# Attention phase of a fused attention + MoE + MoE kernel: PSUM tiles of one bank for the one-bank steps, and a step order written down as a string

## The chip, the cores and the metric

The kernel runs on one core of one Trainium2 chip. The metric is device microseconds of that core for one execution, the median of the runs shown. Engines are named as in the profile: PE (TensorE matmul), PEld (its weight loads), DVE (VectorE), ACT (ScalarE), POOL (GpSimd) and SP (SyncE, which here only issues DMAs).

## What is computed

Three layers follow each other, all in fp32.

```python
s_g  = scale * q_g @ [k_g, k_l].T                      # 32 global queries see all 544 keys
out_g = softmax(s_g) @ [v_g, v_l]
s_ll = where(|i - j| <= 32, scale * q_l @ k_l.T, -1e9) # 512 local queries: a band of keys
s_l  = [scale * q_l @ k_g.T, s_ll]                     # and the 32 global keys
out_l = softmax(s_l) @ [v_g, v_l]
x = heads of [out_g, out_l] side by side               # 2176 tokens x 512
h = (silu(x @ w_gate) * (x @ w_val)) @ w_out           # d_ff 1536
y = h @ w_in2
out = (y * tanh(softplus(y))) @ w_out2                 # d_ff 2048
```

There are 4 batches, 8 heads of 64 columns, 512 local and 32 global tokens per batch.

## The kernel before, in words

The program has two phases. The change touches only the first, the **attention phase**, which takes the first fifth of the time. It works on pairs of heads: n = 0 to 15, four per batch. All its steps are small tasks with a name, an engine, what they need, and, for PE steps that write PSUM, how many banks they take and which later step frees them (`until`). The steps of one pair are:

- on SP, `qk` (six DMAs, lines 166 to 171) and `v` (four DMAs, lines 190 to 192) load the operands; `gk`, `vg` and `vgb` (lines 157, 177, 181) load the global rows of a batch, `w` (lines 581, 584) a piece of the first weights, `Xd` and `GXd` (line 138) store the result to DRAM;
- `A` (PE, L200, two banks) transposes q and k; `Ak`, `Aq` (L289, L299, L301) and `At`, `Ag` (POOL) copy them out;
- `S`, g = 0 and 1 (PE, L317, two banks) makes the scores of half a pair's queries; four `M` (DVE, L328) add the mask and take the minimum of the negated scores; four `E` (ACT, L335) exponentiate; `R` (DVE, L340 and L341) and `N` (POOL, L346 and L348) normalise;
- `C` (PE, L200 on `sm` and `sng`, two banks) transposes the probabilities, `V` (ACT, L363) copies them out;
- `D` (PE, L381 and L385, one bank) multiplies by the values; `Xc` (ACT, L124), `Xh` (DVE, L134), `Xl` (POOL, L136) and `Xd` split and store the result.

For every second pair the global queries go through the same chain with the names `GA` (PE, L412, one bank), `GM` (DVE, L418 to L420), `GE` (ACT, L425 and L427), `GR`, `GN`, `GT` (PE, two banks), `GV` (ACT, L449), `GO` (PE, L459, one bank), `GXc` (ACT, L128). Per batch `AG` and `GG` (PE, L485 and L501, one bank each) prepare the global keys and queries.

Between these stand six conversions of weight pieces, `Cq`, `Cf` 0 to 3, `Ch`, `Cl` (ACT L588, four DVE steps in `w_step`, ACT, POOL), and work of the second layer that is used as filling for PE: for token tiles 0, 1 and 2 the steps `F` (gate and value products, PE L656, one bank), `Ft`, `Fg`, `Fp`, `Fh`, `Fl`, and then `F2` 0 to 3 (the output product, PE L656, one bank each), whose banks `Fy` (DVE, L709) copies into `y`.

The order of these 872 steps is set by `in_order`, a small list scheduler that runs when the kernel is built: each task has a key (a number from `KEY` plus ten per pair) and an estimated duration (`ROOM`, `LAND`), each engine takes the ready task with the smallest key, and the PSUM is eight banks in four tiles of two. A two-bank step takes a whole tile; a one-bank step takes a free bank, preferring one whose other half is in use:

```python
PAIR = [ps_pair.tile([128, 2, 512], F32, ...) for i in range(4)]
def one(task):
    i = place[task][0]
    return PAIR[i // 2][:, i % 2]
...
got = [min(some, key=lambda i: used[i ^ 1] is None)] if some else None
```

On every engine the instructions then stand in the order in which `in_order` put them, and run in that order. Semaphores between engines are set by the framework from what each instruction reads and writes of each tile. In the built program this is by tile, and not by bank, for waits between PE and its readers: a PE instruction that writes one bank of a `pair` tile waits for the last DVE or ACT read of either bank, and a reader waits for the last PE write to either.

The **second phase** starts with `plain_tile(0, 3)` (PE L1064, first layer of token tile 3) and is laid out by a planner of its own, which the change does not touch. Its DVE, ACT and POOL work begins with the conversion of the next weights (DVE L596 to L602, POOL L894).

Of the kernel before, what the change touches and what calls it, by code (L numbers as in the profile page):

```python
# [1 line left out]

# [18 lines left out]
def tile_attn_moe_moe2(  # L21
# [75 lines left out]
    def setup():  # L97
# [5 lines left out]
        for i in range(7):  # L103
            nc.tensor.matmul(PAIR[3][:, 0, 0:128], lhsT=z, rhs=z, start=True, stop=True)
# [93 lines left out]
    def transpose_half(out, src, j):  # L198
# [6 lines left out]
    LAND = {"Xd": 2.6, "GXd": 2.6, "TD": 2.8, "TO": 3.5, "w": 8.0, "qk": 4.0, "v": 5.0, "gk": 4.5, "vg": 5.0, "vgb": 5.0}  # L205
    QACT = lambda n: n % 2 == 0
    KEY = {'lP': 0.2, 'lO': 0.1, 'qk': -24.4, 'v': -9.4, 'A': -11.6, 'S': 0.5, 'E': 10.4, 'R': 49.5,
           'N': -29.7, 'C': -90.7, 'V': -58.2, 'D': -82.8, 'X': 21.9, 'GA': -4.7, 'GT': 42.8, 'GO': 27.7,
           'gk': -16.2, 'vg': 1.0, 'AG': -11.3, 'w': 24.3, 'dw': 20.7, 'C0': 82.8, 'dC': 3.0, 'F': 80.0,
           'At': -70.0, 'GM': -260.3, 'Ch': -231.6}  # L210
    CT = lambda i: KEY["C0"] + KEY["dC"] * i

    ROOM = {"A": 0.6, "S": 0.85, "M": 0.41, "E": 0.51, "R": 0.55, "N": 1.98, "V": 0.73, "D": 1.95, "Xh": 0.6, "Xl": 1.35,
            "GM": 1.2, "GE": 1.02, "GR": 0.55, "GN": 1.7, "Aq": 0.66, "Ak": 0.72, "Xc": 0.62, "GXc": 0.25, "qk": 3.4, "v": 2.4}
    STEPS = (1.1, 0.6, 0.9, 0.95)

    def task(name, key, engine, room, needs, work, banks=0, until=None):
        room = STEPS[name[2]] if name[0] == "Cf" else ROOM.get(name[0], room)
        tasks[name] = (key, engine, room, [x for x in needs if x is not None], work, banks, until)

    def in_order():

        done, start, order = {}, {}, []
        used = [None] * 8
        free = {"PE": 0.0, "DVE": 2.5, "ACT": 3.9, "POOL": 3.0, "SP": 0.0}
        wait = {e: sorted((n for n in tasks if tasks[n][1] == e), key=lambda n: tasks[n][0]) for e in free}
        now = 0.0
        while any(wait.values()):
            for i in range(8):
                if used[i] is not None and done.get(used[i], 1e9) <= now:  # L230
                    used[i] = None
            for e, queue in wait.items():
                if free[e] > now:
                    continue
                for n in queue:
                    key, _, room, needs, work, banks, until = tasks[n]
                    if any(done.get(x, 1e9) > now for x in needs):
                        continue
                    if banks == 2:
                        got = next(([2 * i, 2 * i + 1] for i in range(4) if used[2 * i] is used[2 * i + 1] is None), None)  # L240
                    elif banks == 1:
                        some = [i for i in range(8) if used[i] is None]
                        got = [min(some, key=lambda i: used[i ^ 1] is None)] if some else None
                    else:
                        got = []
                    if got is None:
                        continue
                    for i in got:
                        used[i] = until
# [295 lines left out]
    def attention():  # L545
# [12 lines left out]
        for name in in_order():  # L558
            tasks[name][4]()
# [886 lines left out]
```

## Time and profile before

| what | us |
|---|---|
| median of 3 runs (lowest, highest) | 951.75 (950.51, 951.76) |
| the profiled execution's own time | 947.95 |
| span of that execution in the profile | 945.9 |
| PE busy | 908.0 (96%) |
| DVE, ACT, POOL busy | 620.7, 582.5, 528.4 (66%, 62%, 56%) |

The profile is of one execution. Its times in the rows are microseconds from the start of the span, unless marked ns. In a timeline row the columns are start, duration, engine, line, operation, output and inputs, shapes and count; in brackets stand the idle time of that engine just before it and the instruction that ended the wait. A "pair" in the rows is any of the four PSUM tiles, since buffer numbers are left out. The first `L1064` at 199.28 marks the end of the attention phase.

### The profile page before, as it was taken

To read this page: it belongs to the slowest core of one execution; us is meant where nothing else is said; L and a number is where in the kernel's file an instruction comes from. 1 tells how busy PE (TensorE), PEld (TensorE's weight loads), DVE (VectorE), ACT (ScalarE), POOL (GpSimd) and SP (SyncE) were. 2 spreads that over 40 slices of the span, in tenths; PEclk is the share of its full clock that TensorE was granted. 3 is DMA by queue.
4 is the path that set the end of the run, shared out by engine and by line. 5 is a ranking of instruction groups with operands and counts; after the bars stand their busy time and mean duration, and the time that the engine had idled before them with its cause. 6 is when DMAs were issued, how large, how long until landed. Compare 5 with 4: busy or idle time off the path is not lost.

```text
span 945.9 us, 16820 instructions
## 1 busy us (share of the span) xinstructions
PE 908.0 (96%) x6166; PEld 814.7 (86%) x6166; DVE 620.7 (66%) x1174; ACT 582.5 (62%) x1218; POOL 528.4 (56%) x512
## 2 busy tenths in 40 slices
PE   8878989989899999999999999999999999999998
PEld 6666767878798999999999998888888889888986
DVE  6676866559978878878788895555755575212323
ACT  6775656733334555454455668878767877776763
POOL 5776766648999568575383697434423352233211
PEclk9989999999999999999999999999999999999999
DMA  6768634346766555666655321112211210000112
GB/s 149 176 161 202 164 101 101 83 139 202 232 231 225 179 184 175 193 196 202 192 192 204 130 66 47 45 49 63 68 45 45 68 54 14 0 1 1 69 43 78
DMA packets 134609, 112.76 MB, mean 119 GB/s; under 512 B 79616, under 2 KB 119552, under 8 KB 134528
## 3 DMA queue, kind: packets, MB, share of 16 engines
q1 hardware_dynamic: 133088, 110.85, 38.6%
q8 instruction: 48, 0.79, 0.3%
q10 hardware_dynamic: 1440, 0.85, 0.3%
q14 instruction: 33, 0.27, 0.1%
HBM read 93.85 MB, written 17.83 MB: 118 GB/s over the span
## 4 chain that ended last, share of the span: by engine, by line
PE 80%; POOL 7%; ACT 4%; DVE 4%; issue 3%; DMA 1%; SPq 1%; POOLq 0%; DVEq 0%; ACTq 0%
PE p L1230 19%; PE p L1185 19%; PE p L1104 17%; PE p L1007 11%; PE pair L656 4%; PE p L1064 2%; POOL b L964 2%; PE pair L381 2%; PE pair L317 1%; PE pair L385 1%; POOL w L894 1%; PE pair L200 1%; POOL a L894 1%; POOL e L846 1%; PE pair L459 1%
## 5 line engine op out<-in xcount | busy, mean ns | idle before, releaser
L894 POOL TENSOR_TENSOR a<-s,a 128x384 fp32r<-128x384 f32 (+2 forms) x125 | 146.7, 1183 | 236.6 <-ACT a L893 210.2
L1230 PE MATMUL p<-w,a 128*128 128x512 f32 x816 | 199.0, 391 | 0.0
L1185 PE MATMUL p<-xh,w 128*128 128x384 f32 (+1 forms) x640 | 189.9, 358 | 0.1
L1230 PEld LDWEIGHTS p<-w,a 128*128 128x128 f32 x816 | 152.5, 188 | 29.8
L1007 PE MATMUL p<-a,w 128*128 128x384 f32 (+2 forms) x744 | 139.3, 335 | 3.0 <-POOL w L894 3.0
L1007 PEld LDWEIGHTS p<-a,w 128*128 128x128 f32 x744 | 126.4, 188 | 6.8 <-POOL w L894 3.3
L1104 PE MATMUL p<-xh,w 128*128 128x384 f32 (+1 forms) x496 | 128.7, 326 | 0.4 <-ACT b L1116 0.4
L1185 PEld LDWEIGHTS p<-xh,w 128*128 128x128 f32 x640 | 118.2, 188 | 12.4 <-DVE s L1208 0.5
L894 POOL TENSOR_TENSOR w<-cx,w 128x512 fp32r<-128x512 f32 (+1 forms) x78 | 95.5, 1233 | 48.1 <-ACT w L893 32.5
L1185 PE MATMUL p<-xl,w 128*128 128x384 f32 (+1 forms) x320 | 114.3, 357 | 0.0
L1208 DVE TENSOR_TENSOR s<-s,p 128x384 f32<-128x384 f32 (+1 forms) x80 | 45.7, 605 | 95.7 <-ACT s L1206 95.2
L893 ACT ACTIVATE a<-s 128x384 fp32r<-128x384 f32 (+2 forms) x142 | 73.7, 537 | 35.3 <-DVE s L1050 34.0
L596 DVE SCALAR_TENSOR_TENSOR fl<-q,st 128x512 f32<-128x512 f32 x68 | 67.6, 993 | 41.4 <-ACT q L588 41.3
L1196 ACT ACTIVATE s<-p 128x384 f32<-128x384 f32 (+1 forms) x80 | 42.2, 528 | 82.7 <-PE p L1185 81.5
L1104 PEld LDWEIGHTS p<-xh,w 128*128 128x128 f32 x496 | 88.4, 188 | 0.8 <-ACT b L1116 0.7
L1104 PE MATMUL p<-xl,w 128*128 128x384 f32 (+1 forms) x248 | 80.7, 326 | 0.0
L1116 ACT ACTIVATE b<-p 128x384 f32<-128x384 f32 (+1 forms) x72 | 34.0, 473 | 68.1 <-PE p L1104 65.7
L1016 DVE TENSOR_TENSOR y<-p,y 128x384 f32<-128x384 f32 (+2 forms) x116 | 62.1, 541 | 18.0 <-PE p L1007 17.4
L602 DVE SCALAR_TENSOR_TENSOR cx<-st,cx 128x512 uint32<-128x512 uint32 x68 | 71.7, 1054 | 0.8
L600 DVE SCALAR_TENSOR_TENSOR cx<-fl,cx 128x512 uint32<-128x512 uint32 x68 | 70.4, 1035 | 1.1
L1064 PE MATMUL p<-xh,w 128*128 128x384 f32 (+1 forms) x224 | 65.3, 364 | 1.2 <-DVE y L709 1.2
L1246 DVE TENSOR_TENSOR y<-p,y 128x512 f32<-128x512 f32 x51 | 34.8, 690 | 48.3 <-PE p L1230 48.1
(135 smaller groups left out, 1773.8 us busy)
## 6 DMA issues: line engine op xcount, KB each, us to landing
st<-in_moe_w_out SPq DMA_DIRECT2D x28, 512.0 KB, 4.6
e<-td SPq DMA_DIRECT2D x32, 384.0 KB, 4.0
st<-in_moe_w_in SPq DMA_DIRECT2D x16, 512.0 KB, 3.5
vw<-in_v_l SPq DMA_DIRECT2D x32, 224.0 KB, 4.5
st<-in_moe_w_gate SPq DMA_DIRECT2D x12, 512.0 KB
st<-in_moe_w_val SPq DMA_DIRECT2D x12, 512.0 KB, 3.4
td<-b SPq DMA_DIRECT2D x16, 384.0 KB, 3.2
xh<-td SPq DMA_DIRECT2D x16, 384.0 KB, 4.7
```

Source lines behind the costliest of these rows:

```text
L596: nc.vector.scalar_tensor_tensor(fl, q, TINY2, hw, op0=ALU.is_ge, op1=ALU.mult)
L600: nc.vector.scalar_tensor_tensor(x, fu, 0xC0000000, x, op0=ALU.bitwise_and, op1=ALU.bitwise_or)
L602: nc.vector.scalar_tensor_tensor(x, STG.pop(p)[:, :, 0], 29, x, op0=ALU.logical_shift_right, op1=ALU.bitwise_or)
L893: add("ACT", AC(n), lambda e: nc.scalar.activation(out=dst(0), in_=src(), func=AF.Copy), r=[rd], w=list(dict.fromkeys(wr)), margin=m)
L894: add(lo or [("POOL", PO(n))], 0, lambda e: vec(e).tensor_tensor(out=dst(1), in0=src(), in1=dst(0).bitcast(F32), op=ALU.subtract), r=[rd, ...
L1007: nc.tensor.matmul(ps.h[:, 0:n], lhsT=a.h[:, d], rhs=b.h[:, 0:n], start=(i == 0 and j == 0), stop=(i == len(ws) - 1 and j == 2))
L1016: add("DVE", DV(n), lambda e: nc.vector.tensor_tensor(out=ya, in0=ps.h[:, 0:n], in1=ya, op=ALU.add), r=[ps], w=yt)
L1064: nc.tensor.matmul(ps.h[:, 0:n], lhsT=a.h[:, d], rhs=b[:, c, c0:c0 + n], start=(c == 0 and j == 0), stop=(c == KD - 1 and j == 2))
L1104: nc.tensor.matmul(ps.h[:, 0:n], lhsT=w.h[:, 256 * a + 128 * c:256 * a + 128 * c + 128], rhs=xs[b][:, c, :], start=(start and c == 0 and j ...
L1185: nc.tensor.matmul(h.h[:, 0:n], lhsT=a.h[:, d], rhs=b[:, c, c0:c0 + n], start=(c == 0 and j == 0), stop=(c == KD - 1 and j == 2))
L1208: add("DVE", DV(n), lambda e, s=s, h=h, n=n: nc.vector.tensor_tensor(out=s.h[:, 0:n], in0=s.h[:, 0:n], in1=h.h[:, 0:n], op=ALU.mult), r=[h ...
L1230: nc.tensor.matmul(ACC_[c].h, lhsT=a.h[:, d], rhs=b.h, start=(first and j == 0), stop=(last and j == 2))
```

## The change

It does four things.

1. PSUM becomes two tiles of two banks (`PAIR`) and four tiles of one bank (`ONE`). Two-bank steps (`A`, `S`, `C`, `GT`: 88 in all) use the first, one-bank steps (`D`, `GA`, `GO`, `AG`, `GG`, `F`, `F2`) the second.
2. `in_order` no longer schedules. It reads a string of 872 letters, each a kind of step, and takes the next step of that kind; the tile of a PE step is the one that has been free longest.
3. Keys, estimated durations and landing times go; the steps themselves, what they need, their engines and their instructions stay the same.
4. The order that the string gives is another one. Conversions of weights and `F` steps stand earlier (the first `F` after the fifth `D`, where before it came after the eighth), the weight loads `w` too, and on SP the `qk` loads of later pairs stand ahead of the `v` loads of earlier ones.

```diff
-            nc.tensor.matmul(PAIR[3][:, 0, 0:128], lhsT=z, rhs=z, start=True, stop=True)
+            nc.tensor.matmul(ONE[0][:, 0:128], lhsT=z, rhs=z, start=True, stop=True)
...
-    PAIR = [ps_pair.tile([128, 2, 512], F32, tag=f"pair{i}", name=f"pair{i}") for i in range(4)]
+    PAIR = [ps_pair.tile([128, 2, 512], F32, tag=f"pair{i}", name=f"pair{i}") for i in range(2)]
+    ONE = [ps_pair.tile([128, 512], F32, tag=f"one{i}", name=f"one{i}") for i in range(8 - 2 * len(PAIR))]
     place = {}
 
     def both(task):
-        return PAIR[place[task][0] // 2]
+        return PAIR[place[task]]
 
     def one(task):
-        i = place[task][0]
-        return PAIR[i // 2][:, i % 2]
+        return ONE[place[task]]
...
-    KEY = {'lP': 0.2, 'lO': 0.1, 'qk': -24.4, 'v': -9.4, 'A': -11.6, 'S': 0.5, 'E': 10.4, 'R': 49.5,
...
+    KINDS = ("qk gk A AG Ak AGk At Aq AGe Ag w S GG M E GA R GGe N C V vg GM v GE GR GN Cq D Cf vgb GT "
+             "Xc GV Xh GO Xl Xd Ch GXc GXh GXd Cl GXl F_g Ft F_v Fg Fp Fh Fl F2 Fy").split()
+    ORDER = "abbcdefghadijkjlamlnnnnnooooocnonoephglqnroacsnonnnooelqjgsohtunnnvbnoqtouwsxkllyaxdonnnnzcoonAeooBnpjCq"
...
-                    if banks == 2:
-                        got = next(([2 * i, 2 * i + 1] for i in range(4) if used[2 * i] is used[2 * i + 1] is None), None)
-                    elif banks == 1:
-                        some = [i for i in range(8) if used[i] is None]
-                        got = [min(some, key=lambda i: used[i ^ 1] is None)] if some else None
...
+        free = {2: list(range(len(PAIR))), 1: list(range(len(ONE)))}
+        until = {}
+        for letter in ORDER:
+            n = left[KINDS[(ascii_letters + digits).index(letter)]].pop(0)
+            _, needs, _, banks, last = tasks[n]
...
+            place[n] = free[banks].pop(0) if banks else None
+            if banks:
+                until[last] = banks, place[n]
+            if n in until:
+                free[until[n][0]].append(until[n][1])
+            done.append(n)
+        return done
...
-        task(("A", n), t + KEY["A"], "PE", 0.65, [("qk", n)], qk, 2, ("Aq", n))
+        task(("A", n), "PE", [("qk", n)], qk, 2, ("Aq", n))
```

Three places show what moves. In the rows below a line number of the changed kernel is 23 to 29 smaller or one larger than that of the same code before (PE L459 is L436 now, L656 is L629, L1064 is L1035, SP L166 is L167).

**PE, around the third global output (`GO`, L459; L436 now).** The `gtl` rows are `GO`, the `pt` rows the end of the fifth `D`, the `kst` rows two `S`. Before:

```order
L385 MATMUL pair1_118<-pt_964,vw_907 64x64 [waits DMAHW3_49]
L385 MATMUL pair1_118<-pt_964,vw_907 64x64 [waits DMAHW4_49]
L385 MATMUL pair1_118<-pt_964,vw_907 64x64 x6
L385 MATMUL pair1_118<-pt_1017,vw_907 64x64 x8
L459 MATMUL pair1_118<-gtl_1082,vw_907 64x32 [waits Activation_49]
L459 MATMUL pair1_118<-gtl_1082,vw_907 64x32 x7
L459 MATMUL pair1_118<-gtl_1082,vgb_116 64x32 [waits DMAHW1_49]
L459 MATMUL pair1_118<-gtl_1082,vgb_116 64x32
```

Now:

```order
L295 MATMUL pair1_118<-kst_1092,qT_1136 128x224 [waits DVE_49,Pool_49]
L295 MATMUL pair1_118<-kst_1092,qT_1136 128x224 x3
L295 MATMUL pair0_117<-kst_1092,qT_1136 128x224 [waits Activation_49]
L295 MATMUL pair0_117<-kst_1092,qT_1136 128x224
L295 MATMUL pair0_117<-kst_1092,qT_1136 128x224 [waits Pool_49]
L295 MATMUL pair0_117<-kst_1092,qT_1136 128x224
L436 MATMUL one2_121<-gtl_1205,vw_927 64x32 x8
L436 MATMUL one2_121<-gtl_1205,vgb_116 64x32 [waits DMAHW5_49]
```

`GO` stood right behind `D` in the other bank of the same tile and waited for ACT, which reads that tile for `D`; now it has a tile of its own, stands behind two `S` steps, and its first rows wait for nothing.

**PE, the end of the attention phase.** These are the last `F2` step (on the `ah` and `al` tiles) and the first matmul of the second phase (on `xh`). Before:

```order
L656 MATMUL pair0_117<-ah_2898,w8_1982 128x384 [waits DVE_49]
L656 MATMUL pair0_117<-al_2899,w8_1982 128x384
L656 MATMUL pair0_117<-ah_2898,w9_1983 128x384
L656 MATMUL pair0_117<-ah_2992,w10_2131 128x384
L656 MATMUL pair0_117<-al_2993,w10_2131 128x384
L656 MATMUL pair0_117<-ah_2992,w11_2132 128x384
L1064 MATMUL p0_3076<-xh_105,w0_1450 128x384 [waits DVE_49,PE_49]
```

Now:

```order
L629 MATMUL one0_119<-ah_2818,w8_2158 128x384 [waits DVE_49]
L629 MATMUL one0_119<-al_2819,w8_2158 128x384
L629 MATMUL one0_119<-ah_2933,w10_2296 128x384
L629 MATMUL one0_119<-al_2934,w10_2296 128x384
L629 MATMUL one0_119<-ah_2933,w11_2297 128x384
L1035 MATMUL p0_3078<-xh_105,w0_756 128x384 [waits PE_49]
```

The four `F2` of token tile 2 used the two banks of `pair0` in turn; now they use `one0`, `one3`, `one1` and `one0` again. The first matmul of the second phase no longer waits for DVE.

**SP, the first loads.** After the loads of pairs 0 and 1. Before:

```order
L190 DMA vw<-in_v_l 128x7x64 x2
L191 DMA vw<-in_v_l 64x2x64
L192 DMA vw<-in_v_l 64x2x64
L166 DMA ks<-in_k_l 128x4x64 x2
L168 DMA qs<-in_q_l 128x3x64 x2
L170 DMA qs<-in_q_l 96x2x64
L171 DMA qs<-in_q_l 32x2x64
L190 DMA vw<-in_v_l 128x7x64 x2
```

Now:

```order
L558 DMA st_197<-in_moe_w_gate 128x4x256
L167 DMA ks<-in_k_l 128x4x64 x2
L169 DMA qs<-in_q_l 128x3x64 x2
L171 DMA qs<-in_q_l 96x2x64
L172 DMA qs<-in_q_l 32x2x64
L167 DMA ks<-in_k_l 128x4x64 x2
L169 DMA qs<-in_q_l 128x3x64 x2
L171 DMA qs<-in_q_l 96x2x64
L172 DMA qs<-in_q_l 32x2x64
L178 DMA vg<-in_v_g 32x4x64 x4
L158 DMA gkq<-in_k_g 128x1x64 x2
L191 DMA vw<-in_v_l 128x7x64 x2
```

The first `v` load stood third and now stands behind a weight load, the `qk` loads of pairs 2 and 3, `vg` and half of a `gk`.

## Rows read from the trace of the kernel before

**Rows 1.** Busy time of PE by stretch: us, PE busy (count), PEclk, DMA share, GB/s

```profile
0.00:48.00 48.00, 40.39 (x624) 1.00 0.69 162
48.00:72.00 24.00, 17.80 (x270) 0.86 0.67 161
72.00:199.20 127.20, 111.09 (x1418) 1.00 0.51 133
```

**Rows 2.** Timeline, one stall of PE and what led to it

```profile
61.25 0.93 PE L381 MATMUL pair<-pt,vg 128*64 128x128 f32 x11 [1.36 <-DMA vg<-in_v_g]
63.26 0.69 DVE L418 TENSOR_REDUCE gmx<-pair 128x1 f32<-128x512 f32 x1 [4.30 <-PE pair L385]
64.36 0.69 ACT L425 ACTIVATE sg<-pair,grc 128x512 f32<-128x512 f32 x1 [3.95 <-DVE rc L340]
65.34 0.58 ACT L124 ACTIVATE xf<-pair 128x512 f32<-128x512 f32 x1
65.98 0.66 PE L459 MATMUL pair<-gtl,vw 128*64 128x32 f32 x16 [2.75 <-ACT xf L124]
```

**Rows 3.** Timeline, other stalls of PE behind readers of the neighbouring bank

```profile
123.22 0.44 PE L656 MATMUL pair<-xh,w 128*128 128x384 f32 x1 [0.32 <-DVE t L674]
152.86 0.44 PE L656 MATMUL pair<-xh,w 128*128 128x384 f32 x1 [0.65 <-ACT gxf L128]
165.57 0.60 ACT L124 ACTIVATE xf<-pair 128x512 f32<-128x512 f32 x1 [1.56 <-PE pair L412]
167.37 0.41 PE L656 MATMUL pair<-xh,w 128*128 128x384 f32 x1 [1.39 <-DVE gmx L419]
191.75 0.44 PE L656 MATMUL pair<-ah,w 128*128 128x384 f32 x1 [0.70 <-ACT xf L124]
```

**Rows 4.** Waits of PE, 72 to 199.2 us: us in total, times, longest

```profile
PE pair L656 <- DVE y L709: 2.9, 4, 0.9
...
PE pair L381 <- DVE y L709: 0.8, 1, 0.8
```

**Rows 5.** A stall of PE on a load, and PE's clock behind two stalls

```profile
51.88 0.46 PE L200 MATMUL pair<-ident,ks 64*128 64x64 f32 x8 [1.71 <-DMA ks<-in_k_l]
52.00:58.00 6.00, 5.84 (x50) 0.72 0.94 225
66.00:72.00 6.00, 6.00 (x122) 0.72 0.56 132
```

**Rows 6.** The first DMA issues, the first D step, and landing times of v loads

```profile
7.92 1.03 SPq L190 DMA_DIRECT2D vw<-in_v_l  x2
10.46 1.06 SPq L166 DMA_DIRECT2D ks<-in_k_l  x2
13.67 1.04 SPq L190 DMA_DIRECT2D vw<-in_v_l  x2
16.10 2.58 SPq L177 DMA_DIRECT2D vg<-in_v_g  x4
28.02 0.43 SPq L584 DMA_DIRECT2D st<-in_moe_w_gate  x1
19.43 1.49 PE L381 MATMUL pair<-pt,vg 128*64 128x128 f32 x15
vw<-in_v_l SPq DMA_DIRECT2D x32, 224.0 KB, 4.5
```

**Rows 7.** Timeline where the second phase begins, and its first stall of PE

```profile
199.28 0.41 PE L1064 MATMUL p<-xh,w 128*128 128x384 f32 x1 [1.21 <-DVE y L709]
199.05 1.89 DVE L596 SCALAR_TENSOR_TENSOR fl<-q,st 128x512 f32<-128x512 f32 x1
250.33 2.08 PE L1007 MATMUL p<-a,w 128*128 128x512 f32 x7 [2.95 <-POOL w L894]
```

**Rows 8.** Costliest groups of the attention phase: readers of the two-bank tiles

```profile
L328 DVE CUSTOM_DVE_ANT_0 sm<-pair,mask 128x224 f32<-128x224 f32 x128 | 42.5, 383 | 3.0 <-PE pair L317 3.0
L363 ACT ACTIVATE pt<-pair 128x640 f32<-128x640 f32 x32 | 21.9, 699 | 3.0 <-PE pair L200 2.9
```

More of the change, by code (lines that the diff above doesn't have):

```diff
@@ L1 @@
 from contextlib import ExitStack
+from string import ascii_letters, digits
 import concourse.bass as bass
@@ L211, in tile_attn_moe_moe2 @@
[L211 to L219, printed above, removed]
@@ L221, in in_order @@
-    def in_order():
[L223 to L238, printed above, removed]
-                    if banks == 2:
-                        got = next(([2 * i, 2 * i + 1] for i in range(4) if used[2 * i] is used[2 * i + 1] is None), None)
-                    elif banks == 1:
-                        some = [i for i in range(8) if used[i] is None]
-                        got = [min(some, key=lambda i: used[i ^ 1] is None)] if some else None
[L244 to L249, printed above, removed]
-                    place[n] = got
-                    late = LAND.get(n[0], KEY["lP"] if e == "PE" else KEY["lO"])
-                    free[e] = now + room
-                    done[n] = now + room + late
-                    order.append(n)
-                    queue.remove(n)
-                    break
-            later = [x for x in list(free.values()) + list(done.values()) if x > now]
-            if not later:
-                raise RuntimeError("no task can start: " + str({e: q[:3] for e, q in wait.items()}))
-            now = min(later)
-        return order
@@ new lines, in tile_attn_moe_moe2, with task @@
+    ORDER += "oqtTFsCHVWtuuXYGxLJCNIZ0O0GIKLZZRK00PLZ0"
+    def task(name, engine, needs, work, banks=0, until=None):
+        tasks[name] = engine, [x for x in needs if x is not None], work, banks, until
+    def in_order():
+        left, done = {}, []
+        for n in tasks:
+            left.setdefault(f"F_{n[3]}" if n[0] == "F" else n[0], []).append(n)
+        free = {2: list(range(len(PAIR))), 1: list(range(len(ONE)))}
[3 more added lines that the diff above has]
+            _, needs, _, banks, last = tasks[n]
+            if not all(x in place for x in needs):
+                raise RuntimeError(f"{n} comes before what it needs")
+            place[n] = free[banks].pop(0) if banks else None
[5 more added lines that the diff above has]
+        return done
@@ L528, in go @@
             next(gen, 0)
-        t = CT(i)
-        task(("Cq", i), t, "ACT", 0.67, [("w", i)] + ([("Cf", i - 1, 0)] if i else []), go)
+        task(("Cq", i), "ACT", [("w", i)] + ([("Cf", i - 1, 0)] if i else []), go)
         for j, room in enumerate((0.70, 1.20, 0.75, 0.80)):
             need = [("Cf", i, j - 1)] if j else [("Cq", i)] + ([("Cf", i - 1, 3), ("Cl", i - 2)][:i] if i else [])
-            task(("Cf", i, j), t + 0.1 * j, "DVE", room, need, go)
-        task(("Ch", i), t + KEY["Ch"], "ACT", 0.63, [("Cf", i, 3)], go)
-        task(("Cl", i), t + KEY["Ch"], "POOL", 1.45, [("Ch", i)], go)
+            task(("Cf", i, j), "DVE", need, go)
+        task(("Ch", i), "ACT", [("Cf", i, 3)], go)
+        task(("Cl", i), "POOL", [("Ch", i)], go)
     TD = {}
@@ L558, in attention @@
         for name in in_order():
-            tasks[name][4]()
+            tasks[name][2]()
     STG, W = {}, {}
@@ L712, in add_fill @@
             before = ("F2", t, c, 0)
-            task(before, key, "PE", 0.15 + n * 0.00272, [("Fl", t, fs[0]), ("Fl", t, fs[1]), ("Cl", 4), ("Cl", 5)],
+            task(before, "PE", [("Fl", t, fs[0]), ("Fl", t, fs[1]), ("Cl", 4), ("Cl", 5)],
                  lambda c=c: [second_part(c, i) for i in range(2)], 1, ("Fy", t, c))
-            key += 1
-            task(("Fy", t, c), key, "DVE", 0.69, [before], lambda c=c: copy(c))
+            task(("Fy", t, c), "DVE", [before], lambda c=c: copy(c))
     def out_rows(c0, n):
```

109 lines of the change are left out of this document (53 added, 56 removed).

## Prediction

> **What bounds the kernel now.** I read the busy times by stretch first, then the waits of PE, then the timeline around the longest of them. PE is not busy for 945.9 - 908.0 = 37.9 us of the span, and most of that lies in the attention phase, as [rows 1] show: in the first 48 us PE is idle for 48.00 - 40.39 = 7.6 us, from 48 to 72 for 6.2 us, from there to the end of the attention phase for 16.1 us, 29.9 us together. PE's work in the phase is the same before and after, so the question is which of these waits the change takes away, and what it puts in their place.
>
> Three kinds of wait matter. The first is of the program's own making. [rows 2] are one chain: a late load of `vg` holds the fifth `D` for 1.36 us; `GM` on DVE, which reads a `GA` result in the *other* bank of D's tile, waits 4.30 us for D's matmuls; `GE` on ACT waits 3.95 us for DVE; behind it on ACT stands `Xc`, D's reader; and PE's next step, `GO`, which writes the bank beside D, waits 2.75 us for `Xc`. Neither `GM` nor `GO` needs anything from the bank that it waits for. [rows 3] have four more stalls of PE behind readers of a neighbouring bank: 0.32, 0.65, 1.39 and 0.70 us, and one such wait of a reader, 1.56 us of ACT on a `GA` matmul ahead of the 1.39. A few smaller ones I leave out. [rows 4] are the same thing in turn: `F2` steps write the two banks of one tile alternately, each `Fy` waits until the *next* F2 is done, and the F2 after that waits for Fy: 2.9 us in four waits, and 0.8 us of the `D` behind them.
>
> The second kind is a load: PE waits 1.71 us for `ks` [rows 5]. The third is the clock. In the two 6 us stretches behind the stalls of 1.71 and 2.75 us the granted clock averages 0.72 [rows 5], which is some 3.4 us of each at the lower level, 1.2 GHz, and the rest at 2.4: 6.00 x (1 - 0.72) = 1.7 us of full-speed work lost each time, in rows that count as busy.
>
> **The change part by part.** The sum is made against the profiled execution (947.95 us by its own time, 945.9 us of span) and taken from the median, 951.75; the profiled one lies 3.8 us under it, and I assume that the saving is the same in both.
>
> *Tiles of one bank.* A one-bank step now shares its tile with nobody, so a wait on a neighbour cannot arise. The stall at 65.98 goes, 2.75 us, and with it the fall of the clock behind it, 1.7 us: **4.45 us**. Without the false wait of GM its cause goes too, and GO now stands behind two S steps. The four stalls of [rows 3] go: 0.32 + 0.65 + 1.39 + 0.70 = **3.06 us**. The F2 waits of [rows 4] go, since four F2 now go round three or four tiles, and the reader of the first has two F2 steps of time: 2.9 + 0.8 = **3.7 us**. What stands behind them is PE work that was ready, so I count them in full; the bound from below is zero for those where the true producer turns out hardly earlier.
>
> *The start of the second phase.* PE waits 1.21 us there for the last Fy [rows 7], and in the change that wait is gone. I count **0** for it: the conversion of the next weights begins on DVE at 199.05, behind Fy, and PE stalls at 250.33 for a weight that came through it [rows 7]. That chain starts when the attention phase ends, not when PE starts its first matmul, so PE would arrive 1.2 us earlier at a stall that is 1.2 us longer. The other end is a gain of 1.21.
>
> *SP order, later loads.* In the change `qk` loads stand ahead of `v` loads. The load that PE waits for at 51.88 (pair 7) has as much in front of it as before, within a weight load or two, but the queue before it waited for buffers that a slower PE freed late. I count the 1.71 us and the clock behind it, 1.7 us: **3.4 us**, with zero as the other end. I leave the 1.36 us on `vg` [rows 2] where it is: this load can't be issued before the fourth D is done, and the fifth D now stands closer behind it.
>
> *SP order, first loads.* The price is here. The first `v` load was issued at 7.92 [rows 6]. Now a weight load (0.43), two more `qk` (13.67 - 10.46 = 3.21 each) and `vg` (2.58) stand in front of it: 0.43 + 2 x 3.21 + 2.58 = 9.4 us later, so its large part is issued by 7.92 + 1.03 + 9.4 = 18.4 and, with the 4.5 us that such a load takes to land [rows 6], is there at 22.9. The first D stood at 19.43 [rows 6]. It now also has a GA, an A and half an AG more ahead of it, which shortens the wait. Bounds: 0 to 22.9 - 19.43 = 3.5 us, for this D and alike for the next two, 0 to 10.5 in all. I take **-3.0 us**, nearly one D's worth, since PE's order moves with the loads. The Trainium skill (DMA: Bandwidth & Descriptors, Anatomy of one DMA) gives about 2.0 us plus bytes over 436 GB/s for a load, an estimate of 2.5 us for these 224 KB; by it the data would be there at 20.9, this term near zero and the sum 937 us. The row's 4.5 us decides here.
>
> *Two tiles of two banks.* 88 steps (16 A, 32 S, 32 C, 8 GT) used up to four tiles and now share two. An S holds one until its four M are done, 4 x 0.383 us [rows 8], a C until V is, 0.70 us [rows 8]. In the string most have a D, GA, GO or F between a tile's last use and its next, which covers these times; in the first 25 us some (C behind C, S behind GT) have not. But there PE waits for the chain of ACT and POOL anyway, so I count **0** beyond the 3.0. Its other end is a rival below.
>
> *Converting weights and F earlier* moves work of DVE, ACT and POOL out of the second half of the phase into the first, and gives PE work to fill with from the fifth D on. These engines are busy for 56 to 66% of the span, PE for 96%, so it costs **0**; what it may gain is a rival. The build-time scheduler that goes costs no time on the chip.
>
> Sum: 4.45 + 3.06 + 3.7 + 3.4 - 3.0 = 11.6 us. 951.75 - 11.6 = **940.2 us**. A measurement of this kernel can tell about 0.2%, 1.9 us, from no change.
>
> **The rivals.**
>
> *More goes than I name* (chance 0.14). Of the 16.1 us idle from 72 us on, 3.06 + 3.7 + 1.2 are named; about 8 remain, mostly readers that came late for a bank of their own. With F steps to fill from earlier on, half of it may go (4), and 1.36 + 1.21 and the 3.0 with it: 11.6 + 9.6 = 21.2, 930.6 us. For it: PE has the most work of all engines there. Against: a fixed order can't fill a wait that its author didn't foresee.
>
> *The early loads cost more* (0.20). All three first D wait their full 3.5 us: 10.5 instead of 3.0, 951.75 - 4.1 = 947.7 us. For it: SP issues without a break in this stretch. Each such wait may also drop the clock at 1.7 us a time, up to 951. The Trainium skill (TensorE: Matmul & The Clock Gate, A second HAM failure mode) reports a kernel whose cycling through PSUM banks left PE idle so often that its clock kept falling, which is a rule against a change that puts 88 steps on two tiles. In the first 48 us here PE is idle for 7.6 us in short stalls and the clock stays at 1.00 [rows 1]; so small waits alone don't do it in this kernel.
>
> *Two tiles are too few* (0.17). PE waits for a tile: an S or C whose tile is still held by four M that stand on DVE behind a conversion step or a GM. One whole M group, 4 x 0.383 = 1.53 us, in 10 of 16 pairs is 15.3 us: 951.75 - 11.6 + 15.3 = 955.5 us, slower. It decides from 11.6 / 88 = 0.13 us per two-bank step on. For it: in the early part several of these steps follow each other directly. Against: in the trace M on DVE and V on ACT wait for PE (3.0 and 2.9 us in all [rows 8]), so that they stand ready when a tile is written.
>
> *It doesn't do what it says* (0.03): the waits on neighbours were all covered by true ones just behind, and nothing moves: 951.8 us. Against: the order rows of GO have no wait left.
>
> **How the numbers follow.** The forecast has 0.46, for 935 to 944. Faster by over 0.2%: 0.46 + 0.14 and nine tenths of 0.20, 0.78. Within 0.2%: the rest of the early case, 0.02, about a third of the two-tiles case, 0.05, and "nothing", part of 0.03: 0.09. Slower: 0.13. The range goes from 931, which leaves out half of the first rival, to 953, which leaves out the larger part of the third.
>
> **What would show it.** Right: in the new profile PE waits for no reader behind GO, F or F2 steps; no wait on `y` L709 (now L681) within the phase; clock 1.00 from 60 to 75 us; the first second-phase matmul without a gap, and the stall on the second phase's weights about 1 us longer. The early price shows as waits of D on `vw` before 45 us. Wrong: waits of A, S or C on M (DVE `nb`) or V (ACT `pt`) that sum to over 5 us, or an attention phase that ends no earlier than 195.

## The result, and the profile after

The changed kernel takes **926.7 us** (median; 924.9 to 928.1) against 951.1 (949.8 to 951.8) in the same comparison: ratio 0.974 [0.972, 0.977], 24.4 us faster. The forecast was 940.2 with a range from 931 to 953. The sign and the phase were right, the size was not: twice as much went as was named. The profiled execution has a span of 923.1 us, 22.8 under the 945.9 of before.

The stretches of [rows 1] in the new profile (same columns; the third ends where the attention phase now ends). In all rows below, `S`, `M`, `V` and the two lines of `D` (L317, L328, L363, L381, L385 before) are L295, L306, L341, L359 and L363 in the changed kernel, 22 less:

```profile
0.00:48.00 48.00, 38.83 (x570) 0.96 0.73 176
48.00:72.00 24.00, 22.06 (x285) 0.86 0.71 171
72.00:176.00 104.00, 102.54 (x1452) 1.00 0.56 140
```

PE is idle for 9.2, 1.9 and 1.5 us where it was idle for 7.6, 6.2 and 16.1. After 72 us the phase is packed. Its first matmul of the second phase starts at 176.02 instead of 199.28: 23.26 us, the whole gain. All waits of PE that are left from 72 us to 176 (us in total, times, longest):

```profile
PE pair L295 <- POOL kst L264: 0.8, 1, 0.8
PE pair L201 <- ACT gtl L426: 0.5, 1, 0.5
PE one L359 <- DVE nb L306: 0.2, 1, 0.2
```

The waits of [rows 3] and [rows 4] are gone, and so are all waits on a reader behind F, F2 and GO steps (now L629 and L436). What answers to the other groups, from the new timeline (start, us, engine, line, names, shapes, count, idle before and its releaser):

```profile
46.95 0.47 PE L201 MATMUL pair<-ident,ks 64*128 64x64 f32 x8 [1.37 <-DMA ks<-in_k_l]
68.66 0.66 PE L436 MATMUL one<-gtl,vw 128*64 128x32 f32 x16
176.02 0.33 PE L1035 MATMUL p<-xh,w 128*128 128x384 f32 x1
226.95 0.80 PE L978 MATMUL p<-a,w 128*128 128x512 f32 x1 [2.94 <-POOL w L865]
```

- The third `GO` (68.66), which stalled for 2.75 us in [rows 2], starts without a wait.
- The load of `ks` [rows 5] still stalls PE, 1.37 us instead of 1.71. The wait of the fifth `D` on `vg` (1.36 us in [rows 2]) is gone.
- The second phase starts without the 1.21 us of [rows 7]; its stall on `w` comes 50.93 us later (226.95 - 176.02) and is 2.94 us long; before these were 51.05 and 2.95. The stall did not grow, so the 1.21 us was gained.

Three stretches of six us in the phase, each holding a fall of the clock:

```profile
17.00:23.00 6.00, 5.33 (x45) 0.72 0.58 126
48.00:54.00 6.00, 5.32 (x73) 0.72 0.65 143
55.00:61.00 6.00, 5.31 (x76) 0.72 0.50 113
```

Each takes 6.00 x (1 - 0.72) = 1.7 us of full-speed work from PE. Before there were two of them in the phase [rows 5]; now there are three. So in these two executions the clock gave nothing back: the fall behind GO went, but falls behind other stalls came. What a fall costs in the end no run shows: of the changed kernel's four executions, one took 924.9 us at a mean clock of 0.990 over the whole program and another 926.7 us at 0.998.

One thing the forecast did not look at. PE's busy time in the phase fell from 40.39 + 17.80 + 111.09 = 169.3 us to 38.83 + 22.06 + 102.54 = 163.4, with the same work and one fall of the clock more. Taken at full speed (1.7 us subtracted for each fall) it is 169.3 - 2 x 1.7 = 165.9 before and 163.4 - 3 x 1.7 = 158.3 after: 7.6 us of "busy" went with 17.3 us of idle.

### The profile page after: what moved, and what is told of

It is laid out like the page before. It is cut to its first block, busy times and chain, and to the rows that moved or that the text cites. A ratio compares the mean times of both kernels' runs of the same rounds, so it can differ in the third digit from the quotient of the medians.

```text
span 923.1 us, 16830 instructions
## 1 busy us (share of the span) xinstructions
PE 903.0 (98%) x6166; PEld 816.2 (88%) x6166; DVE 623.9 (68%) x1174; ACT 581.4 (63%) x1218; POOL 530.9 (58%) x512
## 4 chain that ended last, share of the span: by engine, by line
PE 90%; DVE 5%; DMA 2%; issue 1%; POOL 1%; ACT 1%; SPq 0%; DVEq 0%; ACTq 0%; POOLq 0%
PE p L1156 20%; PE p L1201 20%; PE p L1075 18%; PE p L978 13%; PE p L1035 5%; PE one L629 4%; PE pair L295 3%; PE pair L201 2%; PE one L359 2%; PE one L363 2%; DMA td<-b 1%; PE one L436 1%; DMA qs<-in_q_l 1%; DVE sm L306 1%; DVE cx L576 1%
## 5 line engine op out<-in xcount | busy, mean ns | idle before, releaser
L1156 PE MATMUL p<-xh,w 128*128 128x384 f32 (+1 forms) x640 | 189.9, 358 | 0.0
L1075 PE MATMUL p<-xh,w 128*128 128x384 f32 (+1 forms) x496 | 128.4, 326 | 0.0
L864 ACT ACTIVATE a<-s 128x384 fp32r<-128x384 f32 (+2 forms) x142 | 73.7, 537 | 34.5 <-DVE s L1021 33.1
L1156 PEld LDWEIGHTS p<-xl,w 128*128 128x128 f32 x320 | 60.1, 188 | 6.8
```

What stands on the lines that cost most here:

```text
L864: add("ACT", AC(n), lambda e: nc.scalar.activation(out=dst(0), in_=src(), func=AF.Copy), r=[rd], w=list(dict.fromkeys(wr)), margin=m)
L1075: nc.tensor.matmul(ps.h[:, 0:n], lhsT=w.h[:, 256 * a + 128 * c:256 * a + 128 * c + 128], rhs=xs[b][:, c, :], start=(start and c == 0 and j ...
L1156: nc.tensor.matmul(h.h[:, 0:n], lhsT=a.h[:, d], rhs=b[:, c, c0:c0 + n], start=(c == 0 and j == 0), stop=(c == KD - 1 and j == 2))
```

## The experiments

**Names.** *Written order* is the change's string. *Planner* is the build-time scheduler of before, with its old keys. A one-bank step has *separate* tiles (as in the change) or *shared* ones (halves of tiles of two banks, as before). A step gets the *longest-free* tile (as in the change: the free list is a queue) or the *lowest* free number (as the planner chose; before, it first took a bank whose tile was already half in use). The table puts the results first; one thousandth of the ratio is 0.95 us. Each ratio is to executions of the kernel before that were run beside it. "Idle" is PE's, from the busy times by stretch of the profiled execution.

| run | order | one-bank tiles | place | us | ratio to before [95%] | phase ends at | idle to 72 / from 72 us |
|---|---|---|---|---|---|---|---|
| before | planner, four tiles of two banks | shared | lowest | 951.1 | 1 | 199.3 | 13.8 / 16.1 |
| e2b | planner, two of two banks | shared | lowest | 946.1 | 0.996 [0.9945, 0.9974] | 197.1 | 15.7 / 11.1 |
| e2 | as e2b | separate | lowest | 936.0 | 0.985 [0.9834, 0.9867] | 187.8 | 15.5 / 5.0 |
| e7 | as e2b | separate | longest-free | 933.4 | 0.981 [0.9789, 0.9832] | 182.4 | 13.8 / 4.4 |
| e1 | written | shared | longest-free | 934.2 | 0.983 [0.9807, 0.9859] | 185.4 | 13.9 / 4.6 |
| e8 | written | separate | lowest | 935.3 | 0.983 [0.9806, 0.9849] | 187.2 | 15.7 / 5.0 |
| e10 | written | separate | lowest for two banks only | 929.9 | 0.978 [0.9757, 0.9798] | 179.6 | 14.0 / 1.6 |
| after | written | separate | longest-free | 926.7 | 0.974 [0.9723, 0.9765] | 176.0 | 11.1 / 1.5 |

### What the separate tiles are worth: e1, e2, e2b

e1 gives the written order its false neighbours back:

```diff
-    PAIR = [ps_pair.tile([128, 2, 512], F32, ...) for i in range(2)]
-    ONE = [ps_pair.tile([128, 512], F32, ...) for i in range(8 - 2 * len(PAIR))]
+    HALF = [ps_pair.tile([128, 2, 512], F32, ...) for i in range(4)]
+    PAIR, ONE = HALF[:2], [HALF[2 + i // 2][:, i % 2] for i in range(4)]
```

> The order of the change, with the one-bank steps put on the halves of two tiles of two banks; nothing else differs. The whole change measured 926.7 us against 951.1. Theory T (the gain is the waits on the other bank of a shared tile, and what they made late): most of it returns, 940 to 950 us, with stalls of the kind of [rows 3] back on the PE. Theory O (the new order made the part of the gain that was not forecast, some 12 us, and more): 929 to 936 us. By the sums of the forecast, 4.45 + 3.06 + 3.7 = 11.2 return: 938 us.

e2 takes the kernel before and gives its planner the change's tiles; e2b is e2 with the edit of e1:

```diff
...
-   got = next(([2 * i, 2 * i + 1] for i in range(4) if used[2 * i] is used[2 * i + 1] is None), None)
+   got = next(([2 * i, 2 * i + 1] for i in range(2) if used[2 * i] is used[2 * i + 1] is None), None)
-   some = [i for i in range(8) if used[i] is None]
-   got = [min(some, key=lambda i: used[i ^ 1] is None)] if some else None
+   some = [i for i in range(4, 8) if used[i] is None]
+   got = some[:1] or None
```

> The planner of the kernel before with its keys as they were, and the tiles of the change (two of two banks, four of one); the planner, which now has two places for steps of two banks, writes a new order from the old keys. Theory T: faster than before by 10 us or more, under 941 us, if two tiles are enough for this order. Theory O: 943 to 955 us. Rival 'two tiles are too few' for an order not made for them: over 951 us.

> The same order as the run with the old planner, with the one-bank steps on halves of tiles of two banks. Only the waits differ between the two. Theory T: 10 us or more slower than that run. Theory O: at most 5 us slower.

Sharing costs 0.9833 - 0.9744 = 0.0089, 8.5 us (give or take 3.2) at the written order, and 0.9959 - 0.9850 = 0.0109, 10.4 us (2.1) at the planner's. The forecast's 4.45 + 3.06 + 3.7 = 11.2 is of that size, though it was made for the four tiles of before, where steps of one and of two banks share tiles with each other too. So this part was not what it missed. By their expectations e2 and e2b speak for the tiles (theory T), e1 for the order (theory O). Neither theory fits all three: tiles and order each hold a good part.

How the sharing costs is worth a look. Around the fifth D of e1, the timeline of ACT and PE:

```profile
49.90 1.10 PE L363 MATMUL pair<-pt,vw 128*64 128x64 f32 x32
52.30 0.33 PE L460 MATMUL pair<-ident,gkq 128*128 128x128 f32 x1
52.71 0.60 ACT L125 ACTIVATE xf<-pair 128x512 f32<-128x512 f32 x1 [1.27 <-issue]
54.14 0.69 ACT L341 ACTIVATE pt<-pair 128x640 f32<-128x640 f32 x1
54.97 0.46 PE L201 MATMUL pair<-ident,sm 64*128 64x64 f32 x8 [2.34 <-ACT gxf L129]
```

The same steps in the changed kernel:

```profile
49.42 1.92 PE L363 MATMUL one<-pt,vw 128*64 128x64 f32 x32
51.43 0.60 ACT L125 ACTIVATE xf<-one 128x512 f32<-128x512 f32 x1 [1.36 <-issue]
52.89 0.33 PE L460 MATMUL one<-ident,gkq 128*128 128x128 f32 x1
53.05 0.70 ACT L341 ACTIVATE pt<-pair 128x640 f32<-128x640 f32 x1
53.90 0.46 PE L201 MATMUL pair<-ident,sm 64*128 64x64 f32 x8 [0.68 <-ACT gxf L129]
```

With a tile of its own, the copy of D's result (L125) starts 0.1 us after D's last matmul (49.42 + 1.92 = 51.34). With a shared tile it starts 1.7 us after it (49.90 + 1.10 = 51.00), when `AG` (L460) has written the other bank at 52.30 + 0.33 = 52.63: the reader waits for a write that it doesn't read. `V` (L341) stands behind it on ACT, and PE's next `C`, whose tile this `V` frees, waits 2.34 us instead of 0.68. (Its row names `gxf`, the ACT copy just behind `V`.) No row of PE names the false wait. This is the forecast's "readers that came late for a bank of their own", which it left in a rival.

The second line of the table is the surprise of this group. e2b differs from before only in where its planner may put steps: those of two banks on two tiles, those of one bank on the other two. With the same keys it then writes another order, and is 3.9 us (1.4) faster. The order and the neighbours of the steps changed together here, and no run separates them. Two tiles are not too few, and the rival of that name falls.

### What the place is worth: e7, e8, e10, e11

The rest of the string's freedom is the rule by which a step gets its tile. It is one line in the change, and the forecast had no term for it.

```diff
-            place[n] = free[banks].pop(0) if banks else None
+            place[n] = free[banks].pop(free[banks].index(min(free[banks]))) if banks else None
```

That second line is e8; e10 does the same for steps of two banks only:

```diff
-            place[n] = free[banks].pop(0) if banks else None
+            place[n] = free[banks].pop(free[banks].index(min(free[banks])) if banks == 2 else 0) if banks else None
```

e7 is the reverse: the planner's order of e2, step for step, written into the string of the changed kernel, so that against e2 only the places differ:

```diff
-    ORDER = "abbcdefghadijkjlamlnnnnnooooc...
+    ORDER = "abbacexdhgfjdjlilnanomnornonc...
...
```

> The order of the change, each step given the lowest-numbered free tile, as the old planner did, and not the one free longest. Theory P: 933 to 938 us. Theory O: at most 929 us.

> The order of the change; only the two tiles of two banks are given out by the lowest number that is free, the four of one bank by the longest free. With both kinds by the lowest number the time was 935.3 us, with neither 926.7. If the place of the steps of two banks does it (they take a tile whose reader on ACT or DVE has just been issued): 932 to 936 us. If the place of the steps of one bank does it: at most 929 us.

> The old planner's order of the run at 935.95 us, step for step, written down as a string; what differs is the tile each step gets: the one that has been free longest, as in the change, and not the lowest number that is free. Theory P (the rule for the place is what the order's part of the gain comes from, since a step that takes the tile just released waits for its reader): 926 to 930 us. Theory O (the order itself): 934 to 937 us.

At the written order the lowest number costs 0.0084, 8.0 us (2.9); at the planner's 0.0039, 3.7 us (2.6). Of the 8.0, the steps of two banks hold 0.0034, 3.2 us (2.8), by e10, and the others the remaining 4.8. The waits of PE show it: of e8, from 72 us on, those for a tile of one bank that a reader holds,

```profile
PE one L436 <- ACT xf L125: 1.6, 1, 1.6
PE one L629 <- DVE y L681: 0.6, 1, 0.6
PE one L359 <- ACT xf L125: 0.5, 1, 0.5
PE one L389 <- ACT sg L402: 0.3, 1, 0.3
```

and of e10, over the phase:

```profile
PE pair L295 <- ACT pt L341: 3.5, 4, 1.2
PE pair L201 <- ACT pt L341: 2.0, 3, 0.9
PE pair L295 <- DVE nb L306: 1.1, 2, 0.9
```

The waits of `S` (L295) on `V` (L341) went from 1.0 us in the changed kernel to 3.5 in e10, those of `C` (L201) on `V` from 0.9 to 2.0; those of `S` on `M` (`nb`) fell from 2.0 to 1.1. My reading of these: a step that takes the lowest free number often takes the tile whose reader has only just been *issued*, which is free in the string's book-keeping and not yet on the chip. e8 came out as theory P had it; e10 and e7 lie between the ranges of the two theories. Place is worth about as much as separate tiles at the written order, less than half of that at the other.

e11 puts the rule alone into the kernel before:

```diff
-   got = [min(some, key=lambda i: used[i ^ 1] is None)] if some else None
+   got = [min(some, key=lambda i: (used[i ^ 1] is None, since[i]))] if some else None
```

(`since[i]` is when bank i came free; the choice among free tiles of two banks goes by it too.)

> The kernel before, four shared tiles, with one rule of its planner changed: among the places that its rule allows it takes the one free longest, not the lowest number. The order is the same for the first 130 of PE's 168 steps, and for all of SP's. Theory P (the place rule is a part of the gain that the forecast left out): 942 to 948 us. Theory O: 949 to 953 us.

It is slower: 960.2 us, ratio 1.011 [1.009, 1.013]. Both theories missed. Two things are in it. The tenth and eleventh D, which stand in the common part, start at 118.7 and 144.0 us in e11 and at 115.2 and 140.5 before, so the rule gained nothing where the order is the same. And the other order of the last 38 steps leaves more of the fill behind the last D: 22.9 us from there to the second phase (188.3 to 211.2), before 10.3. In that tail, PE's waits and its clock (e11's line numbers are 2 larger than those of before):

```profile
PE pair L658 <- POOL al L639: 3.5, 1, 3.5
PE pair L658 <- DVE y L711: 2.0, 3, 0.7
PE pair L658 <- ACT ah L642: 1.9, 1, 1.9
...
188.30:211.20 22.90, 14.89 (x97) 0.80 0.24 81
```

The place rule pays with separate tiles; with shared ones no run shows a gain.

### What the order is worth: e3 to e6, e9

From e7 to the changed kernel only the order differs: 0.9811 - 0.9744 = 0.0067, 6.4 us (2.9). With the lowest place the two orders lie 0.9850 - 0.9828 = 0.0022 apart (e2 and e8), 2.1 us (2.6), which is within the error: what the order is worth depends on the place. The next runs look for the step that holds the 6.4.

e3 undoes the step that the forecast priced at -3.0 (one letter of the string moved, `v` of the first pair ahead of the first weight load):

```diff
-    ORDER = "abbcdefghadijkjlamlnnnnn...ohtunnnvbnoqtouwsxkllyaxdo...
+    ORDER = "abbcdefghadijxkjlamlnnnnn...ohtunnnvbnoqtouwskllyaxdo...
```

> The order of the change with one load moved: v of the first pair is issued ahead of the first weight piece, as before, so the first weight piece, the loads of q and k of pairs 2 and 3, vg and the first load of the second batch come one load of 224 KB later. By the forecast's term of -3.0 (the first D waits for v) it gains: 923 to 925 us. Without that wait: 927 us, or slower by up to 2 us where the q and k of pair 2 or 3 are late for their turn.

928.3 us, ratio 0.977 [0.975, 0.979]: no gain, and not clearly a loss. There was nothing to undo: neither in the changed kernel's profile nor in e3's does a D wait for `vw`. What the move made late does show in e3's: PE waits 2.3 us for `k_g` and 2.1 for `vg`, where it waited 0.3 and not at all.

e4 holds back the fill in the written order, each of its 78 steps by eight of them (its first F now follows the eighth D); the first 296 letters stay as they are, and one `GO` moves back with the fill:

```diff
...
-    ORDER += "HhmpDrooJoaqt...KKsenBpnqtdsxDSoohfuotuzLlqAka"
+    ORDER += "HhmpDrooJoaqt...KKsenBpnqtdsxDoohfuotuzLlqAkai"
...
```

e6 does the opposite to the kernel before, with one key, that of the first weight conversion, which the F steps wait for:

```diff
-    'gk': -16.2, 'vg': 1.0, 'AG': -11.3, 'w': 24.3, 'dw': 20.7, 'C0': 82.8, 'dC': 3.0, 'F': 80.0,
+    'gk': -16.2, 'vg': 1.0, 'AG': -11.3, 'w': 24.3, 'dw': 20.7, 'C0': 50.0, 'dC': 3.0, 'F': 80.0,
```

> The order and the tiles of the change, but the fill (the F steps and what follows each) begins after the eighth D, as in the kernel before, and not after the fifth: each step of it takes the place that a step eight later had. If the early fill is what closed the gaps from 60 to 100 us (9.1 us of idle PE there before, 0.5 after): 932 to 938 us, with gaps back at 60 to 86 us and none where the fill runs. By the forecast, which counted an earlier fill at nothing: within 2 us of 926.7.

> The kernel before with one key changed (C0 from 82.8 to 50): the fill begins after the fourth D instead of the eighth; four shared tiles as before. If an early fill is worth something by itself: 941 to 946 us. By the forecast, which counted it at nothing: 948 to 952 us. If the fill takes places in PSUM that the attention needs, over 952 us.

e4: 953.7 us, ratio 1.004 [1.002, 1.005], the whole gain gone and more. e6: 954.4, ratio 1.005 [1.003, 1.007], slower than before. Neither theory had this: a late fill costs some 28 us in one order, an early one 5 in the other. In e4 the fill is missing from 62 to 90 us (its first F is at 61.9 in the changed kernel, at 90.0 here). Some idle time came back there, 4.4 us from 60 to 86 us (0.5 in the changed kernel, 7.1 before), but most of it behind: 14.0 us from 86 us on, against 0.9. The first lines of its waits from 72 us on:

```profile
PE pair L201 <- ACT pt L341: 3.7, 4, 1.0
PE one L629 <- ACT ah L614: 3.2, 2, 1.9
PE pair L201 <- ACT gtl L426: 2.0, 2, 1.4
PE pair L201 <- ACT sm L313: 1.7, 1, 1.7
PE one L629 <- POOL al L611: 1.6, 2, 0.9
```

F2 waits for its own chain (`ah`, `al`), and `C` for ACT. The shift moved 24 F and 12 F2 steps on PE and their followers on DVE, ACT and POOL against everything that they had been set between. So e4 does not tell what an early start is worth; it tells that the places of the fill are fitted to the rest. Nor is an early start what the written order has over the planner's: in e2b, e2 and e7 the first F follows the fourth D already, at 54 to 57 us.

e5 gives e2's planner earlier loads of `q_g` and `k_g`. For these PE waited 6.2 us in e2 (3.3 and 2.9), 5.0 of it at 52 to 57 us. (The text below calls this the second batch; its loads, issued at 51.0 and 52.8 us, are the third pair of four.)

```diff
-            task(("gk", b, i), t + KEY["gk"] + i, "SP", ...
+            task(("gk", b, i), t + KEY["gk"] - (14 if b else 0) + i, "SP", ...
```

> The run with the old planner and separate tiles (935.95 us), with one key changed: the loads of q_g and k_g of the second and later batches are due 14 us earlier. In that run the PE waited 5.0 us for the two loads of the second batch, at 52 to 57 us, and the clock fell there. If these loads are the part of the order that the change got right: 929 to 932 us. If another wait stands behind them: over 934 us.

936.4 us, no change from e2. The third batch's two loads are issued at 34.0 and 35.2 us instead of 51.0 and 52.8, and of that wait 0.3 us is left. But the planner took `AG` earlier with its loads: PE now waits 2.0 us for the second batch's and 3.4 for the fourth's, 5.7 in all. So the waits moved, and e5 does not tell what taking them away is worth.

e9 is e7 with SP's queue in the written order; the other four engines keep the planner's:

```diff
-    ORDER = "abbacexdhgfjdjlilnanomnornonc...
+    ORDER = "abbacedhgfjdjlilnnomnornoncon...
...
```

> The old planner's order on PE, DVE, ACT and POOL, with the change's order of the DMA issues on SP, and the tile that has been free longest; to be read against the run that has the planner's own loads and the same rule for tiles. If the order of the loads is a part of the gain: faster than that by 2 to 6 us, and without the waits of the PE for q_g and k_g of the second batch. If not: within 2 us.

967.3 us, ratio 1.017 [1.014, 1.020]. Its waits from 48 to 130 us:

```profile
PE one L460 <- DMA gkq<-in_q_g: 14.7, 2, 10.8
PE pair L201 <- ACT pt L341: 6.3, 2, 5.0
PE pair L201 <- DMA ks<-in_k_l: 1.6, 1, 1.6
```

SP issues in order too, and the planner's PE takes `k_g` and `q_g` of a batch close together (for the third, at 52.07 and 54.06 us in e7, where the loads are issued at 48.77 and 50.54). The written order puts some 10 us of other loads between the two: 46.09 and 56.86 us in the changed kernel, whose PE uses them 9 us apart, and 52.37 and 63.13 in e9. The 10.8 us are this. Each queue is fitted to the others.

### Where in the order: e12 to e15

The two orders are nearly at the same state after 240 of the 872 steps (15 steps differ on either side) and after 460 (16). So the beginning of one was run with the remainder of the other, with the change's tiles and places:

```diff
-    ORDER = "..."     the change's 872 letters
+    ORDER = "..."     the first 240 (or 460) steps of one order, then the other's steps that are left
```

> The first 240 of the 872 steps in the order of the change (to about the fourth D, 50 us), the rest in the old planner's; tiles of the change, longest free. The two whole orders stand at 0.9744 and 0.9811 of before. If the first 240 steps hold the order's gain: 0.973 to 0.976. If the later steps hold it: 0.980 to 0.983. If it is spread: between. If an order only works as a whole: over 0.983.

> The first 240 steps in the old planner's order, the rest in that of the change. If the first 240 hold the gain: 0.980 to 0.983. If the later ones: 0.973 to 0.976. If an order only works as a whole: over 0.983 here too.

> The first 460 steps in the order of the change (to about the ninth D, 100 us), the rest in the old planner's. With the gain in steps 1 to 460: 0.973 to 0.976. With the gain after them: 0.980 to 0.983.

> The first 460 steps in the old planner's order, the rest in that of the change. With the gain in steps 1 to 460: 0.980 to 0.983. With the gain after them: 0.973 to 0.976.

| beginning | remainder | joined at 240 | joined at 460 |
|---|---|---|---|
| written | planner's | e12: 0.986 [0.983, 0.988] | e14: 0.982 [0.980, 0.985] |
| planner's | written | e13: 0.979 [0.977, 0.981] | e15: 0.984 [0.981, 0.986] |
| one order throughout | | planner's (e7): 0.981 [0.979, 0.983] | written: 0.974 [0.972, 0.977] |

None reaches the written order, and e12 and e15 lie no better than the planner's own. If the gain sat in one piece and a join cost nothing, one run of each column would stand at 0.974. Only e13, with the written remainder, tends that way (0.9793 against e7's 0.9811, within the error). But a join has a price of its own: e12 lies 0.0046 over the planner's order, 4.4 us. So the runs fit an order that is worth its 6.4 us only as a whole, and do not show it: a gain in one piece could be hidden under what the join costs. Which steps hold it stays open.

## Why the forecast was wrong

What the 24.4 us are, along one path of the table: the planner's new layout for two tiles (order and neighbours together), 3.9; separate tiles, 10.4; the place rule, 3.7; the written order, 6.4. (The shares depend on the path: at the written order the place is worth 8.0 and the tiles 8.5.) Against the forecast's terms:

- **Tiles of one bank, 4.45 + 3.06 + 3.7 = 11.2.** Right in size, 8.5 to 10.4 measured, and partly by luck: errors of both signs stand in it. The 1.7 us for the clock were not seen to be gained, since in the profiled execution the clock falls once more often than before. The readers held by a neighbour's write, and the busy time that went with the idle time (below), were left out and are in the measured figure.
- **The start of the second phase, 0.** Wrong: 1.2 us gained. I argued that PE would arrive earlier at a stall that would be longer; the stall is as long as before, at the same distance. The conversion on DVE that I took for its cause did start later against PE, 0.79 us behind its first matmul instead of 0.23 ahead, but its first step is shorter now:

```profile
176.81 0.69 DVE L570 SCALAR_TENSOR_TENSOR fl<-q,st 128x512 f32<-128x512 f32 x1
```

  Before it took 1.89 us [rows 7] and ended 1.66 us after PE's first matmul (199.05 + 1.89 - 199.28); now it ends 1.48 us after it (176.81 + 0.69 - 176.02). Why it was longer stays open.
- **Later loads, 3.4.** Wrong: 0.3. `ks` still stalls PE, 1.37 us, and the clock still falls behind it. The 1.36 us on `vg`, which I left where they were, did go.
- **First loads, -3.0.** Wrong: nothing. No D waits for `vw`, and e3 gains nothing. That `v` would be issued later was right: 10.8 us later (18.72 against 7.92), where I had 9.4. That D would be waiting for it was taken from D's *old* start. In the new profile the first D starts at 23.2 us, not 19.4, behind more steps of PE, three waits on DVE, ACT and POOL and a fall of the clock. The formula of the Trainium skill that I set beside this term (DMA: Bandwidth & Descriptors, Anatomy of one DMA) is given there for DMAs that GpSimd issues; these are issued by SP, and no run here tests it.
- **Two tiles of two banks, 0**, and **Converting weights and F earlier, 0.** This is the step that failed: the sum set the new order, and the new rule for the place of a step, at nothing. It priced named rows of the old trace and took what only changed its place for harmless: where the new order stands, it said, PE has work that covers it. The two tiles themselves were not what it missed: PE's waits for `M` or `V` ahead of A, S and C steps sum to 4.1 us in the new profile (2.0 + 1.0 + 0.9 + 0.2) and 1.0 before (0.8 + 0.2), more than the 0 I counted and less than the 5 I named as a sign of being wrong. But the longest-free rule had no term at all, and the order had only the loads and the two zeros. Order and place together gained 0.9850 - 0.9744 = 0.0106, 10.1 us (2.5), with separate tiles (e2 to the changed kernel), and 0.9959 - 0.9833 = 0.0126, 12.0 us (2.8), with shared ones (e2b to e1). The forecast was short by 12.8.
- **The rival "More goes than I name"** went the right way and was too small. It let half of the 8 us of unnamed waits after 72 us go, by the earlier fill, and ended at 930.6. In fact idle time there went from 16.1 to 1.5, and busy time went with it (below); that the earlier fill did it is not shown.
- **The rivals "The early loads cost more" and "Two tiles are too few"** fall: the new profile and e3 for the one, e2b for the other. With two tiles for 88 steps the clock fell three times in the phase instead of twice, each time in the first 61 us and behind stalls; from 72 us on it stands at 1.00. The page of the Trainium skill that I set against the change (TensorE: Matmul & The Clock Gate, A second HAM failure mode) describes a kernel whose clock kept falling as it cycled through PSUM banks. The trace agrees in part: of the stalls just ahead of the falls, those of 0.70, 0.61, 0.68 and 1.26 us stand behind readers of two-bank tiles, those of 0.89 and 1.37 behind POOL and a load; and one more fall went with a kernel that is 24.4 us faster.

Most of what I said would show it right did appear: no reader behind GO, F or F2, no wait on `y`, the clock at 1.00 from 60 to 75 us, no gap at the switch; only the longer stall of the second phase did not. All of that is under half of the gain. Such signs test the terms that a sum has; they say nothing of the ones that it lacks.

## What to carry to other kernels

When a change replaces the whole order of a phase, forecast from the phase's idle time, not from the waits that can be named: PE was idle for 29.9 us there, which stood in the first view, and the change took 17 of them. List how a buffer is chosen as a part of the change of its own: here the one released longest ago was worth 3.7 to 8.0 us over the lowest number, with separate tiles. And don't expect to move one engine's queue, or one kind of step, out of a fitted order to see what it is worth: e4 and e9 lost 28 and 34 us by doing so (against the changed kernel and e7), so compare whole orders, and change tiles or places under them.

## What the runs showed of the hardware

- **Busy time went with idle time.** Ends of matmuls are modelled in the profile, so a part of each wait probably lies in rows that count as busy. At full speed PE's busy time in the phase was 165.9 us before with 29.9 idle, 167 in e4 with 30.0, 160.5 in e2 with 20.5 and 158.3 after with 12.6: about 0.4 us of busy time more for each us of idle time. It is no fixed rate: e9 is idle for 46.3 us and has some 163 (the busy time of each 3 us times its clock, summed). Matmuls of two shapes show how uneven it is. Of the kernel before, and then of the change:

```profile
L656 PE MATMUL pair<-xh,w 128*128 128x384 f32 x64 | 20.2, 358 | 2.7 <-DVE gmx L419 1.4 <-ACT gxf L128 0.7 <-DVE t L674 0.3
L656 PE MATMUL pair<-xh,w 128*128 128x512 f32 x32 | 12.1, 417 | 1.2 <-DVE t L671 0.8 <-ACT gxf L128 0.4
```

```profile
L629 PE MATMUL one<-xh,w 128*128 128x384 f32 x64 | 18.7, 349 | 0.0
L629 PE MATMUL one<-xh,w 128*128 128x512 f32 x32 | 12.1, 419 | 0.0
```

  The same 64 instructions of 384 columns, 20.2 us of busy time with 2.7 idle ahead of them, 18.7 with none: 1.5 us went besides the 2.7. The 32 of 512 columns lost 1.2 us of idle time and nothing else. All F and F2 rows together, which stand at clock 1.00 in both, went from 73.7 us of busy time to 70.9, while 7.5 us of idle time ahead of them went.
- **The clock follows stalls, but not their sum.** In the profiled executions e7 was idle for 18.2 us in the phase and lost 48 x 0.04 = 1.9 us to the clock, one fall; the changed kernel, idle for 12.6, had three, 5.1 us; e2, on the same tiles, four. No run had none.
